# Checks of a DFT matrix by accumulating transfers, and gate weights kept in PSUM, in a Fourier-mixing and product-key expert kernel

## The chip, the cores and the metric

The kernel runs on one core of a Trainium2 chip. The metric is the device time of one execution in microseconds, and the median over executions is compared. The engines are TensorE (PE, with PEld for its weight loads), VectorE (DVE), ScalarE (ACT), GpSimd (POOL) and SyncE (SP). In this program SP issues nearly all transfers, in the order of its queue; POOL issues the transfers that add to what lies at their destination.

## What is computed

```python
xn = layernorm(x)                                  # 2048 x 512
a = einsum("bsd,ed->bse", xn, dft_hid_re)
b = einsum("bsd,ed->bse", xn, dft_hid_im)
y = einsum("ts,bse->bte", dft_seq_re, a) - einsum("ts,bse->bte", dft_seq_im, b)
q = einsum("nd,dhc->nhc", xn, w_q)                 # 32 heads, 2 x 128
s1, s2 = q1 . k1, q2 . k2                          # 64 keys each, top 2 of each
cand = t1[:, None] + t2[None, :]                   # top 2 of the 4 pairs, g = softmax
eidx = i1 * 64 + i2                                # one of 4096 experts
act = gelu(xn . u[eidx])
out = sum over heads and picks of g * act * v[eidx]
result = x + y + out
```

All matrices are inputs. The kernel uses the symmetries of the DFT matrices to load and multiply a quarter of them, and checks on the chip that the inputs have these symmetries. Where a check fails, it computes the general way at the end.

## The kernel before

A first part (to about 163 us) computes the Fourier mixing and stores its rows `y` in DRAM. A second part (to about 406 us) computes scores for eight chunks of heads and finds the two best keys of each half. The third part, which the change is in, goes through all 4096 experts for each of the 16 tiles of 128 tokens. Its phases alternate:

- **z**: `u` times the tokens gives one value for each expert and token, in PSUM, and gelu of it is written to `act`. From tile 2 on two tiles are done together, with seven products in place of eight. A list of 28 such products (`SEQ`, each 24 matmuls of 128 columns) sets their order. What comes out of each is copied by ACT (L1225, L1230, L1232), added by DVE (L1227, L1235, L1238) and passed through gelu by ACT (L1215). Three of the 28 are placed ahead of the phase, between the matmuls of the v phase before, and one behind it.
- **gates**: for 32 tokens at a time (`tg`, four per tile) DVE builds one-hot matrices `L` (L1279) and `R` (L1284, L1287), in three pairs of buffers, and PE multiplies them (L1289) into two banks `g`, of which there are two pairs. `w_part` then multiplies `act` by the gate (DVE, L1297) into an SBUF tile `w`, rounds it to f16 (ACT, L1304; in some places DVE, L1302) and keeps the rest as a second f16 number (DVE, L1305). Both halves overwrite `act`.
- **v**: for each tile, 16 groups of experts in eight slots, 12 matmuls of 512 columns each, add the output (L1349). Seven of the 16 groups of `v` come from DRAM in three buffers in turn.

The phases run z(0), z(1), v(0), then z(2,3), v(1), v(2), z(4,5), v(3), v(4) and so on. A z phase of a pair has 16 slots, a v phase 8. A table `plan` says what follows in program order behind the matmuls of each slot: `put(phase, slot, ...)`, with G for the gates' matmuls and W for `w_part`. A scheduling layer may move instructions against each other on an engine where nothing depends on it, except those that `pin` keeps in program order.

Between these phases lie the **checks**, which fill otherwise idle time and need nothing from the main work:

- 64 comparisons of C, the sequence DFT matrices. `compare` loads a base block of 128 x 128 and seven blocks of the same size that must equal it up to sign (448 KB, L1378). `compare_in` sums the base's magnitudes (DVE, L1385), subtracts or adds it (L1391, L1393, L1404), then mirrors (L1410). ACT sums the magnitudes of what is left over seven blocks (L1430). 16 of the 64 (those with `g == 0`) have special first rows.
- 4 comparisons of the hidden DFT matrices (`compare_w`, DVE L1457 to L1478, ACT L1480).
- 60 sums (`fit`) over weights, either loaded for it (L1488, L1496) or lying in SBUF (L1500), all on ACT.

Comparisons, loaded sums and the tiles `w` share one ring of four SBUF buffers (`WB = 4`). A comparison moves on by one stage with each slot that has a `U` or `F` in the plan:

```python
def step(it):
    for q in (later, loaded) if it is not None else (later, loaded, later):
        ready = q[:]
        del q[:]
        for f in ready:
            f()
    f = None if it is None else next(it, None)
```

The rows of `y` are loaded behind a v phase by SP (L1359), `x` is added by an accumulating transfer from POOL (L1360), DVE adds the scaled output (`finish`, L1364), and SP stores the result (L1365).

Of the kernel before, what the change touches and what calls it, by code (L numbers as in the profile page):

```python
# [36 lines left out]
def tile_fnet_peer(ctx, tc, x, ca, cb, c5, wt, wf, wr, wq, kt, ut, vn, out):  # L37
# [683 lines left out]
    def part_b(safe, stS, stP, stQ, stE, xt, u_sb, cmp_p, w4):  # L721
# [363 lines left out]
        WB = 4  # L1085
# [174 lines left out]
        GP = {}  # L1260

# [6 lines left out]
        def g_mm(b, tg):  # L1268
            cmp = CMP[b]
            p = pg(f"g{b}_{tg}")  # L1270
            for hf in range(2):
                ts = slice(tg * TG + hf * 16, tg * TG + hf * 16 + 16)

                def bc(w, n):
# [4 lines left out]
                nc.vector.tensor_tensor(  # L1279
                    L.rearrange("p t (l two) -> p t l two", two=2),  # L1280
                    io_lam.rearrange("p (l two) -> p l two", two=2).unsqueeze(1).to_broadcast([P, 16, P // 2, 2]),
                    bc(0, P), op=ALU.is_equal)
# [4 lines left out]
                nc.vector.tensor_tensor(Rv, Rv, bc(2, NC), op=ALU.mult)  # L1287
                for t in range(16):
                    nc.tensor.matmul(p[:, hf, t * NC:(t + 1) * NC], L[:, t, :], R[:, t, :], start=True, stop=True)  # L1289
            GP[b, tg] = p  # L1290

        def w_part(b, tg, here=False):
# [3 lines left out]
            w = bp.tile([P, NC, TG], F32, tag="w", name=f"w{b}_{tg}", bufs=WB)  # L1296
            nc.vector.scalar_tensor_tensor(w, act[:, :, ts], fw,  # L1297
                                           p.rearrange("p h (n c) -> p c (h n)", c=NC),
                                           op0=ALU.mult, op1=ALU.mult)
# [56 lines left out]

        def add_x(b):
            Y[b] = y = bp.tile([P, D], F32, tag="y", name=f"y{b}", bufs=1)
            nc.sync.dma_start(y, y_d[b])  # L1359
            nc.gpsimd.dma_start(y, x[b % 4, b // 4], accum_op=ALU.add)  # L1360

        def finish(b, pv):
            y = Y[b]
            nc.vector.scalar_tensor_tensor(y, pv, osc, y, op0=ALU.mult, op1=ALU.add)  # L1364
            nc.sync.dma_start(out[b * P:(b + 1) * P], y)  # L1365

        later, loaded = [], []
        pin = tc.keep_in_program_order

        def compare(n):  # L1370

            ri, g, kk = n // 32, n // 8 % 4, n % 8
            odd = kk // 4
            t = bp.tile([P, 4, 4, 64], F32, tag="w", name=f"cx{n}", bufs=WB)
            tf = t.rearrange("p s q c -> p (s q c)")
            tv = t.rearrange("p s q c -> p s (q c)")
            nc.sync.dma_start(tf[:, :P], ca[ri, g, :, kk * P:(kk + 1) * P])
            nc.sync.dma_start(tf[:, P:], cb[ri, g, kk].rearrange("p b c -> p (b c)"))  # L1378
            loaded.append(lambda: compare_in(n, t, tf, tv))

        def compare_in(n, t, tf, tv):

            ri, g, kk = n // 32, n // 8 % 4, n % 8
# [46 lines left out]
            later.append(lambda: pin(nc.scalar.activation(tf[:, P:], tf[:, P:], AF.Abs, accum_out=chk[:, n:n + 1])))  # L1430

        def compare_w(n):
# [3 lines left out]
            if n == 64:  # L1436
                r = bp.tile([P, 192], F32, tag="zb", name="wr")[0:1, 0:129]
                nc.sync.dma_start(r, wr)
                v = r[:, 2:128].rearrange("p (c a) -> p c a", a=2)
                pin(nc.vector.tensor_tensor(v, v, w2[0:1].unsqueeze(1).to_broadcast([1, 63, 2]), op=ALU.subtract))  # L1440
                nc.vector.tensor_tensor(r[:, 128:129], r[:, 128:129], w2[0:1, 1:2], op=ALU.subtract)
                later.append(lambda r=r: pin(nc.scalar.activation(r[:, 2:129], r[:, 2:129], AF.Abs, accum_out=chk[0:1, 70:71])))
            t = bp.tile([P, 4, 256], F32, tag="w", name=f"cx{n}", bufs=WB)
# [5 lines left out]
            loaded.append(lambda: compare_w_in(n, t))  # L1449

        def compare_w_in(n, t):

            ri, half = divmod(n - 64, 2)
            v = [t[:, k] for k in range(4)]
# [24 lines left out]
            f = t.rearrange("p k e -> p (k e)")[:, P - half * ri:]  # L1479
            later.append(lambda: pin(nc.scalar.activation(f, f, AF.Abs, accum_out=chk[:, n:n + 1])))  # L1480

        def fit(n):

            if n < NK:
                t = bp.tile([P, 2 * D], F32, tag="w", name=f"fit{n}", bufs=WB)
                nc.sync.dma_start(t.rearrange("p (h k) -> p h k", h=2), wq[1 + n // 4, n % 4 // 2, n % 2])
                loaded.append(lambda: later.append(
                    lambda: pin(nc.scalar.activation(t, t, AF.Abs, accum_out=fits[:, n:n + 1]))))  # L1488
                return
            g = n - NW  # L1490
            t = bp.tile([P, 2 * D], F32, tag="w", name=f"fit{n}", bufs=WB)
            if g >= 16 + V2:
                h = t.bitcast(F16)[:, 0:2 * D]
                nc.sync.dma_start(h, v_d[g - 16 - V2, :, 0:2 * D])
                loaded.append(lambda: later.append(
                    lambda: pin(nc.scalar.activation(h, h, AF.Abs, accum_out=fits[:, n:n + 1]))))  # L1496
                return
            src = (u_sb[g][:, 0].rearrange("p c k e -> p (c k e)") if g < 16 else
                   v_sb[g - 16][:, 0].rearrange("p c d -> p (c d)"))
            pin(nc.scalar.activation(t, src, AF.Abs, accum_out=fits[:, n:n + 1]))  # L1500

        def verdict():
# [37 lines left out]
        fit_units = [iter([lambda n=n: fit(n) for n in ns]) for ns in (  # L1540
            (*range(NK), *range(NW + 16 + V2, NW + 32)), range(NW, NW + 16 + V2))]
        units = iter([lambda n=n: (compare if n < 64 else compare_w)(n) for n in range(68)])

        def step(it):
            for q in (later, loaded) if it is not None else (later, loaded, later):
                ready = q[:]
                del q[:]
                for f in ready:
                    f()
            f = None if it is None else next(it, None)  # L1550
            if f is not None:
                f()
# [301 lines left out]
```

## Time and profile before

| | |
|---|---|
| time, median of 3 runs | 1132.39 us (1127.87 to 1136.62) |
| the profiled execution's own time | 1135.25 us |
| its span, first to last instruction | 1133.4 us |
| PE busy | 1107.3 us (98%) |
| DVE busy | 962.7 us (85%) |
| ACT busy | 663.9 us (59%) |
| POOL busy | 332.7 us (29%) |
| moved by DMA | 220.51 MB |
| mean granted clock of TensorE | 0.995 |

The span is 1.9 us shorter than the time of the same execution. Lines of the profile begin with `L` and the line of the kernel. A row of the view by lines ends with the busy time, the mean of one instruction in ns, and the idle time of the engine just ahead of these instructions with what ended it. In the view of waits each row gives the sum, the number and the longest.

### The profile page before, as it was taken

The numbers are of one execution on the slowest core, as the hardware profiler recorded it, in microseconds if no ns is written. First come the engines' busy times: TensorE is split into PE (matmuls) and PEld (weight loads), VectorE is DVE, ScalarE is ACT, GpSimd is POOL, SyncE is SP. The second block draws the span as 40 slices with busy tenths as digits, with TensorE's granted clock in tenths as the row PEclk, the third lists the DMA queues.
The fourth block names the chain that finished last, engine by engine and source line by source line (L and its number), as shares of the span: only waits on it lengthen the run. The fifth ranks groups of instructions, "written<-read, shape, count | busy, mean of one in ns | idle before, by whom it ended". The sixth has DMA issues, their size and how long they took to land.

```text
span 1133.4 us, 29112 instructions
## 1 busy us (share of the span) xinstructions
PE 1107.3 (98%) x11528; PEld 722.5 (64%) x11528; DVE 962.7 (85%) x2904; ACT 663.9 (59%) x1098; POOL 332.7 (29%) x385
## 2 busy tenths in 40 slices
PE   9999999999999999999999999999999999999997
PEld 6455554544545459687488478478569569569643
DVE  7899789999989799948997897898888888888793
ACT  6558598888877584346445545544535545544442
POOL 0429999899888850000000000000000000000000
PEclk9999999999999999999999999999999999999999
DMA  9883546465353335866666777666668668566354
GB/s 291 292 206 148 185 139 223 117 217 170 92 168 96 111 108 191 236 199 205 226 206 226 227 218 241 218 207 232 200 205 263 199 211 269 190 221 206 121 168 134
DMA packets 132273, 220.51 MB, mean 195 GB/s; under 512 B 35092, under 2 KB 71067, under 8 KB 132126
## 3 DMA queue, kind: packets, MB, share of 16 engines
q1 hardware_dynamic: 129520, 214.28, 58.7%
q0 software_dynamic: 2304, 4.20, 2.8%
q8 instruction: 92, 1.51, 0.5%
q14 instruction: 55, 0.45, 0.1%
q10 hardware_dynamic: 302, 0.08, 0.0%
HBM read 183.06 MB, written 29.69 MB: 188 GB/s over the span
## 4 chain that ended last, share of the span: by engine, by line
PE 59%; DVE 15%; DMA 5%; ACT 4%; issue 2%; POOL 1%; SPq 0%; ACTq 0%; DVEq 0%
PE s L252 18%; PE z L1186 17%; PE v L1349 16%; PE z L1108 4%; DMA cx<-in_cb_dram 3%; DVE w L1297 3%; DVE L L1279 3%; PE g L1289 3%; DVE act L1305 2%; PE m L148 1%; DVE R L1287 1%; DVE R L1284 1%; DVE w L1305 1%; DMA s<-s_d 1%; DVE cx L1393 1%
## 5 line engine op out<-in xcount | busy, mean ns | idle before, releaser
L252 PE MATMUL s<-m,xq 128*128 128x512 f16 x1344 | 297.4, 379 | 1.7 <-ACT ss L962 1.4
L1349 PE MATMUL v<-v,act 128*128 128x512 f16 x1044 | 233.3, 379 | 0.0
L252 PEld LDWEIGHTS <-xq 128*128 128x128 f16 x1344 | 129.6, 98 | 153.1 <-issue 3.2
L1360 POOL DMA_DIRECT2D y<-in_x_dram x16 | 14.4, 897 | 658.7 <-DMA v<-v_d 274.7
L1279 DVE TENSOR_TENSOR L<-io_lam,cmp 128x2048 f16<-128x2048 f16 x128 | 156.2, 1221 | 28.1 <-PE g L1289 28.1
L1349 PEld LDWEIGHTS <-act 128*128 128x128 f16 x1044 | 99.2, 98 | 112.4
L1186 PEld LDWEIGHTS <-u 128*128 128x128 f16 x2688 | 156.2, 98 | 14.8 <-issue 8.3
L966 DVE MAX8 vals<-ss 128x8 f32<-128x64 f32 x896 | 133.3, 216 | 5.5 <-ACT ss L962 5.2
L1186 PEld LDWEIGHTS <-s 128*128 128x128 f16 x1944 | 110.6, 98 | 1.2 <-DMA s<-s_d 1.2
L1349 PE MATMUL v<-v,w 128*128 128x512 f16 x480 | 109.0, 384 | 0.0
L1304 ACT ACTIVATE act<-w 128x1024 f16<-128x1024 f32 x36 | 48.9, 1358 | 92.2 <-DVE w L1297 92.2
L970 DVE FIND_INDEX8 idx<-vals,ss 128x8 uint16<-128x256 f32 x224 | 93.7, 418 | 0.0
L962 ACT ACTIVATE ss<-s,wsc 128x512 f32<-128x512 f32 x120 | 80.0, 680 | 22.5 <-PE s L252 12.6
L1186 PE MATMUL z<-xb,u 128*128 128x128 f16 x1344 | 84.9, 220 | 5.3 <-DVE w L1227 4.7
L1186 PE MATMUL z<-x,u 128*128 128x128 f16 x1344 | 84.7, 220 | 1.6 <-DVE act L1238 1.1
L1186 PE MATMUL z<-x,s 128*128 128x128 f16 x1296 | 81.2, 219 | 1.0 <-DMA s<-s_d 1.0
L1215 ACT ACTIVATE act<-act,scl 128x512 f32<-128x512 f32 x56 | 39.6, 720 | 70.9 <-DVE act L1235 40.9
L1349 PEld LDWEIGHTS <-w 128*128 128x128 f16 x480 | 46.1, 99 | 53.1 <-issue 2.3
L1430 ACT ACTIVATE cx<-cx 128x896 f32<-128x896 f32 x64 | 60.0, 938 | 29.6 <-DVE cx L1410 11.7
L1289 PEld LDWEIGHTS <-L 128*128 128x128 f16 x2048 | 60.7, 96 | 17.3 <-issue 7.2
L1289 PE MATMUL g<-R,L 128*128 128x32 f16 x2048 | 63.5, 177 | 6.6 <-DVE R L1287 6.2
L1305 DVE TENSOR_TENSOR act<-w,act 128x1024 f16<-128x1024 f32 x44 | 58.6, 1332 | 6.1 <-ACT act L1304 6.1
(363 smaller groups left out, 1878.9 us busy)
## 6 DMA issues: line engine op xcount, KB each, us to landing
v<-v_d SPq DMA_DIRECT2D x67, 512.0 KB, 4.6
s<-s_d SPq DMA_DIRECT2D x63, 512.0 KB, 4.2
cx<-in_cb_dram SPq DMA_DIRECT2D x64, 448.0 KB, 5.7
w<-in_wq_dram SPq DMA_DIRECT2D x28, 512.0 KB, 5.9
fit<-in_wq_dram SPq DMA_DIRECT2D x28, 512.0 KB, 4.3
uv<-in_vn_dram SPq DMA_DIRECT2D x16, 512.0 KB
uv<-in_ut_dram SPq DMA_DIRECT2D x16, 512.0 KB, 3.5
s_d<-v SPq DMA_DIRECT2D x32, 256.0 KB, 2.5
```

The source lines that it names most:

```text
L252: nc.tensor.matmul(ps, xt[i][:, l, kd, :], m[:, r, kd, :], start=(n == 0), stop=(n == 3 * KD - 1))
L962: nc.scalar.activation(s, ps, AF.Copy, scale=inv)
L966: nc.vector.max(vals[:, i, w, :, h], s[:, g, :])
L970: nc.vector.max_index(idx[:, i, w].rearrange("p k h -> p (k h)"), vals[:, i, w, 0:2].rearrange("p k h -> p (k h)"), s[:, w * HC:g + 1, :]. ...
L1108: nc.tensor.matmul(ps if n == 1 else ps.rearrange("p (b n) -> p b n", b=2), ug[:, l, c % 2, kd, :], xb2[:, k0, r, kd, :] if n == 1 else xb ...
L1186: nc.tensor.matmul(bank[:, t * P:(t + 1) * P], lt, rt, start=(t == k == 0 and op in "125"), stop=(t == 3 and k == 5), skip_group_check=op ...
L1279: nc.vector.tensor_tensor(L.rearrange("p t (l two) -> p t l two", two=2), io_lam.rearrange("p (l two) -> p l two", two=2).unsqueeze(1).to_ ...
L1289: nc.tensor.matmul(p[:, hf, t * NC:(t + 1) * NC], L[:, t, :], R[:, t, :], start=True, stop=True)
L1304: nc.scalar.activation(w16[..., 0], w, AF.Copy)
L1305: nc.vector.tensor_tensor(w16[..., 1], w, w16[..., 0], op=ALU.subtract)
L1349: nc.tensor.matmul(pv, w16[:, c, :, l], v_sb[g][:, r, cc, :], start=(n + cc == 0 and k == 0), stop=(n == end and cc == 1 and k == 2))
L1430: later.append(lambda: pin(nc.scalar.activation(tf[:, P:], tf[:, P:], AF.Abs, accum_out=chk[:, n:n + 1])))
```

## The change

**The comparisons.** For 48 of the 64 comparisons of C (those with `g` not 0) DVE no longer subtracts. `base_load` brings the base block alone into a small tile `cb` (three buffers). `expect` lets DVE sum its magnitudes (L1411) and lets ACT write the negated expectation of all seven blocks into the check's tile, in one to four instructions by a table of signs (`SETS`, L1418; a few more of one column each where `kk == 0`, L1422). Then POOL issues an accumulating transfer that adds the seven blocks of the input on top (L1423). `sum_up` sums the magnitudes of the result on ACT (L1428). The other 16 and the four of the hidden matrices work as before.

**The weights.** `w` is no longer an SBUF tile: L1307 writes the product back into the gates' own PSUM banks, and the rounding (L1312, L1310) and the rest (L1313) read it there. So a pair of banks is in use until the rest is taken. The ring of four buffers holds checks alone (`CB = 4`, tag `cx`).

**The building of L and R** is a function of its own (`g_prep`), put into the plan as `LRP` one to three slots ahead of its matmuls; G and W have new slots.

**A table of times.** The steps of a check are put at slots by a table: 2.1 us are counted for a slot of z and 3.0 us for a slot of v. The base is loaded 7 us ahead of `expect`, and the sum taken 9 us behind it. A comparison of the old kind is computed 8 us behind its load and summed 12 us behind. The 128 checks are spread evenly over the slots. `load_y`, `add_x` and `store` have slots of their own too.

```diff
-        def g_mm(b, tg):
+        def g_prep(b, tg):
...
-            p = pg(f"g{b}_{tg}")
...
+                PREP.setdefault((b, tg), []).append((L, R))
+                pin(nc.vector.tensor_tensor(
...
+        def g_mm(b, tg):
+            if (b, tg) not in PREP:
+                g_prep(b, tg)
+            p = pg(f"g{b}_{tg}")
+            for hf, (L, R) in enumerate(PREP.pop((b, tg))):
...
-            w = bp.tile([P, NC, TG], F32, tag="w", name=f"w{b}_{tg}", bufs=WB)
-            nc.vector.scalar_tensor_tensor(w, act[:, :, ts], fw,
-                                           p.rearrange("p h (n c) -> p c (h n)", c=NC),
-                                           op0=ALU.mult, op1=ALU.mult)
+            w = p.rearrange("p h (n c) -> p c (h n)", c=NC)
+            nc.vector.scalar_tensor_tensor(w, act[:, :, ts], fw, w, op0=ALU.mult, op1=ALU.mult)
...
+        def load_y(b):
+            Y[b] = bp.tile([P, D], F32, tag="y", name=f"y{b}", bufs=1)
+            pin(nc.sync.dma_start(Y[b], y_d[b]))
+
         def add_x(b):
-            Y[b] = y = bp.tile([P, D], F32, tag="y", name=f"y{b}", bufs=1)
-            nc.sync.dma_start(y, y_d[b])
-            nc.gpsimd.dma_start(y, x[b % 4, b // 4], accum_op=ALU.add)
+            pin(nc.gpsimd.dma_start(Y[b], x[b % 4, b // 4], accum_op=ALU.add))
...
+        SETS = {(0, 0): ((-1, 0, ((7, 1),)),),
...
+        def base_load(n):
+
+            ri, g, kk = n // 32, n // 8 % 4, n % 8
+            b = T[n, "b"] = bp.tile([P, 132], F32, tag="cb", name=f"cb{n}", bufs=3)
+            nc.sync.dma_start(b[:, :P], ca[ri, g, :, kk * P:(kk + 1) * P])
+            if kk == 0:
+                nc.sync.dma_start(b[:, P:P + 1], cb[ri, g, 0, :, 0, 0:1])
+
+        def expect(n):
...
+            t = T[n] = check_tile(f"cx{n}")[:, 0:7 * P].rearrange("p (h c) -> p h c", h=7)
+            pin(nc.vector.tensor_reduce(asum[:, n:n + 1], b[:, :P], axis=AX.X, op=ALU.add, apply_absolute_value=True))
+            for sign, at, dims in SETS[ri, kk // 4]:
...
+                pin(nc.scalar.activation(v, src.to_broadcast([P, *[k for k, step in dims], P]), AF.Copy, scale=float(sign)))
...
+            pin(nc.gpsimd.dma_start(t.rearrange("p h c -> p (h c)"), cb[ri, g, kk].rearrange("p b c -> p (b c)"),
+                                    accum_op=ALU.add))
+
+        def sum_up(n):
+            f = T.pop(n).rearrange("p h c -> p (h c)")
+            pin(nc.scalar.activation(f, f, AF.Abs, accum_out=chk[:, n:n + 1]))
...
-                put(ph, 1, G(b + 1, 0))
+                put(("v", b - 1), 7, LRP(b + 1, 0))
+                put(ph, 1, G(b + 1, 0), LRP(b + 1, 1))
...
-                for k in range(4):
-                    put(ph, 2 * k or b % 2, W(b + 1, k))
-                put(ph, b % 2, G(b + 1, 2))
-                put(ph, 3, G(b + 1, 3))
...
+                put(ph, 3, G(b + 1, 2), LRP(b + 1, 3))
+                put(ph, 4, W(b + 1, 2), G(b + 1, 3))
+                put(ph, 6, W(b + 1, 3))
...
+            kinds = [[((timed(base_load, n), -7.0), (timed(expect, n), 0.0), (timed(sum_up, n), 9.0))
+                      for n in range(64) if n // 8 % 4],
```

Two places in the built order. The first is DVE where v(7) ends and v(8) begins: `y` is the finish of v(7), L and R (with `cmp`) belong to the gates of tile 9, `cx` and `cb` to checks, `g_3` and `w_126` to the last weights of tile 8. Before:

```order
L1385 TENSOR_REDUCE sums<-cx_12484 128x1
L1418 COPY cx_12456<-cx_12456 1x128
L1391 TENSOR_TENSOR cx_12484<-cx_12484 128x256
L1393 SCALAR_TENSOR_TENSOR cx_12484<-cx_12484,not_79 128x256
L1287 TENSOR_TENSOR R_5773<-R_5773,cmp_12414 128x512
L1395 TENSOR_TENSOR cx_12484<-cx_12484 1x256
L1410 TENSOR_TENSOR cx_12484<-cx_12484 128x128
L1410 TENSOR_TENSOR cx_12484<-cx_12484 1x128
L1364 SCALAR_TENSOR_TENSOR y_12510<-v_12228,scl,y_12510 128x512
L1418 COPY cx_12484<-cx_12484 1x128
L1279 TENSOR_TENSOR L_5774<-io_lam,cmp_12414 128x2048
L1284 TENSOR_TENSOR R_5775<-io_c,cmp_12414 128x512
```

The same place on DVE in the changed kernel:

```order
L1307 SCALAR_TENSOR_TENSOR g_3_12403<-w_126,scl,g_3_12403 128x32x32
L1291 TENSOR_TENSOR R_5773<-R_5773,cmp_12378 128x512
L1283 TENSOR_TENSOR L_5774<-io_lam,cmp_12378 128x2048
L1313 TENSOR_TENSOR w_126<-g_3_12403,w_126 128x32x32
L1411 TENSOR_REDUCE sums<-cb_12440 128x1
L1283 TENSOR_TENSOR L_5772<-io_lam,cmp_12378 128x2048
L1291 TENSOR_TENSOR R_5775<-R_5775,cmp_12378 128x512
L1288 TENSOR_TENSOR R_5777<-io_c,cmp_12378 128x512
L1291 TENSOR_TENSOR R_5777<-R_5777,cmp_12378 128x512
L1373 SCALAR_TENSOR_TENSOR y_12297<-v_12232,scl,y_12297 128x512
L1283 TENSOR_TENSOR L_5776<-io_lam,cmp_12378 128x2048
L1283 TENSOR_TENSOR L_5772<-io_lam,cmp_12378 128x2048
```

Both halves of L and R for the first gates of tile 9 now stand ahead of the finish, and the operations of the comparison that stood there are gone but for one sum of the base.

The second place is ACT at the end of z(12,13): `z_12` are the banks of that phase, `act` the results of its two tiles, `w_0` or `g_0` the first weights, `cx` checks. Before:

```order
L1215 ACTIVATE act_14121<-act_14121,scl 128x4x128
L1232 ACTIVATE act_14299<-z_12_0_14726 128x4x128
L1215 ACTIVATE act_14121<-z_12_2_14532,scl 128x4x128
L1430 ACTIVATE cx_14792,sums<-cx_14792 128x896
L1215 ACTIVATE act_14299<-act_14299,scl 128x4x128 x2
L1215 ACTIVATE act_14121<-z_12_0_14726,scl 128x4x128
L1304 ACTIVATE act_14121<-w_0_15141 128x32x32
L1430 ACTIVATE cx_14971,sums<-cx_14971 128x896
```

The same place on ACT in the changed kernel, where `cb` is a base block:

```order
L1232 ACTIVATE act_14275<-z_12_0_14733 128x4x128
L1215 ACTIVATE act_14111<-z_12_2_14523,scl 128x4x128
L1428 ACTIVATE cx_14727,sums<-cx_14727 128x896
L1418 ACTIVATE cx_15094<-cb_14981 128x2x2x128
L1418 ACTIVATE cx_15094<-cb_14981 128x128
L1418 ACTIVATE cx_15094<-cb_14981 128x2x128
L1215 ACTIVATE act_14275<-act_14275,scl 128x4x128 x2
L1428 ACTIVATE cx_14881,sums<-cx_14881 128x896
L1428 ACTIVATE cx_15094,sums<-cx_15094 128x896
L1215 ACTIVATE act_14111<-z_12_0_14733,scl 128x4x128
L1312 ACTIVATE act_14111<-g_0_14759 128x32x32
```

One sum stood between two gelus of the phase's end; now three sums and three writes of an expectation stand there, and the last two sums wait for accumulating transfers.

More of the change, by code (lines that the diff above doesn't have):

```diff
@@ L1644, in part_b @@
[L1644 to L1649 removed]
+            slots = [(ph, cg) for ph in phases[2:] for cg in range(16 if len(ph) == 3 else 8)][:-5]
+            at = [0.0]
+            for ph, cg in slots:
+                at.append(at[-1] + (2.1 if ph[0] == "z" else 3.0))
@@ L1650, in part_b @@
+            put(("z", 1), 3, timed(load_y, 0))
+            put(("z", 1), 6, timed(add_x, 0))
         ZP = {}
```

204 lines of the change are left out of this document (120 added, 84 removed), and 3 rows, old and new, of the table SETS.

## The prediction

> **What bounds the kernel now.** I read the page first, then the waits of PE, then the timeline around its longest gaps, then the granted clock beside them.
>
> ```profile
> span 1133.4 us, 29112 instructions
> PE 1107.3 (98%) x11528; PEld 722.5 (64%) x11528; DVE 962.7 (85%) x2904; ACT 663.9 (59%) x1098; POOL 332.7 (29%) x385
> ...
> PE g L1289 <- DVE R L1287: 6.2, 10, 2.2
> PE z L1186 <- DVE w L1227: 4.7, 3, 2.4
> PE z L1186 <- DVE act L1238: 1.1, 1, 1.1
> PE z L1186 <- DMA s<-s_d: 1.0, 1, 1.0
> PE z L1186 <- DVE act L1235: 0.6, 2, 0.3
> PE z L1186 <- DVE act L1227: 0.3, 1, 0.3
> PE z L1186 <- DVE w L1235: 0.2, 1, 0.2
> ```
>
> PE is busy 98% of the span, and the change removes no matmul. So only PE's idle time can be won. In the third part PE waits 6.2 + 4.7 + 1.1 + 0.6 + 0.3 + 0.2 = 13.1 us for DVE, and 1.0 us for a load of `s`. It never waits there for ACT. Two of the longest waits, from the timeline:
>
> ```profile
> 773.11 0.88 DVE L1393 SCALAR_TENSOR_TENSOR cx<-cx,not 128x256 f32<-128x256 f32 x2 [2.08 <-DMA cx<-in_cb_dram]
> ...
> 774.37 0.67 DVE L1238 TENSOR_TENSOR act<-z,w 128x512 f32<-128x512 f32 x1
> ...
> 775.17 0.67 DVE L1227 TENSOR_TENSOR w<-z,w 128x512 f32<-128x512 f32 x1
> ...
> 775.89 1.50 PE L1186 MATMUL z<-xb,u 128*128 128x128 f16 x24 [1.97 <-DVE w L1227]
> ...
> 819.16 0.73 DVE L1364 SCALAR_TENSOR_TENSOR y<-v,scl,y 128x512 f32<-128x512 f32 x1
> ...
> 823.02 0.55 PE L1289 MATMUL g<-R,L 128*128 128x32 f16 x16 [2.24 <-DVE R L1287]
> ```
>
> In the first, DVE stands 2.08 us in front of a check whose transfer has not landed; two additions of z banks are queued behind it, and PE needs the bank. In the second the gates' R is late, since a run of comparisons and the finish stood ahead of it (the first order above). Both are DVE's queue, not DVE's total.
>
> ```profile
> 556.00:568.00 12.00, 10.19 (x93) 5.13 (x90) 11.35 (x21) 4.93 (x9) 0.86 (x1) 0.86 0.85 286
> 1040.00:1044.00 4.00, 3.85 (x66) 3.85 (x66) 1.68 (x4) 3.31 (x6) 0.00 (x0) 0.60 0.19 75
> 932.00:967.00 35.00, 35.00 (x690) 34.92 (x687) 29.82 (x49) 19.26 (x32) 0.86 (x1) 1.00 0.72 232
> ```
>
> Each row is a window with its length, the busy time of PE, PEld, DVE, ACT and POOL, and then the granted clock. Behind two of the waits the clock is granted in part: 12 x 0.14 = 1.7 us and 4 x 0.40 = 1.6 us are lost, 3.3 us in all. The Trainium skill, "TensorE: Matmul & The Clock Gate", Part 1, lets the clock drop only after an idle window of about 3.4 us. The trace differs: its longest wait is 2.4 us, and the clock fell. By the page the 3.3 us would not be on offer; I go by the rows.
>
> So what is on offer is 13.1 + 3.3 = 16.4 us, and 1.0 us of DMA.
>
> **DVE's share of the checks.** The subtractions and mirrors of 48 comparisons go:
>
> ```profile
> L1404 DVE TENSOR_TENSOR cx<-cx 128x512 f32<-128x512 f32 x36 | 24.6, 684 | 7.6 <-DMA cx<-in_cb_dram 7.6
> L1404 DVE TENSOR_TENSOR cx<-cx 128x256 f32<-128x256 f32 x36 | 15.0, 417 | 0.7 <-DMA cx<-in_cb_dram 0.7
> L1404 DVE TENSOR_TENSOR cx<-cx 128x768 f32<-128x768 f32 x12 | 11.4, 951 | 3.0 <-DMA cx<-in_cb_dram 3.0
> L1410 DVE TENSOR_TENSOR cx<-cx 128x128 f32<-128x128 f32 x56 | 15.7, 283 | 0.1
> ```
>
> All of L1404 is theirs, 24.6 + 15.0 + 11.4 = 51.0 us, and 42 of the 56 mirrors, 11.9 us: 63 us of DVE, with 11.3 us of waits for transfers. This is time beside PE, so it counts only through the 13.1 us. Twenty comparisons stay on DVE with their operations in one piece, now computed 8 us by the table behind their load. The waits of z phases behind checks sum to 4.7 + 1.1 + 0.6 + 0.3 + 0.2 = 6.9 us; I leave 20/68 of that, 2.0 us. Of the gates' 6.2 us I leave 0.6, since `LRP` puts all of L and R ahead of the finish, as the order shows. Gain: 13.1 - 2.6 = 10.5 us, and the 3.3 us of clock, as no wait near 2 us is left. The bounds are 0 and 16.4 us.
>
> **Weights in PSUM.** The three steps for one quarter tile, in the timeline:
>
> ```profile
> 546.81 1.27 DVE L1297 SCALAR_TENSOR_TENSOR w<-w,scl,g 128x1024 f32<-128x1024 f32 x1
> 548.12 1.35 ACT L1304 ACTIVATE w<-w 128x1024 f16<-128x1024 f32 x1 [4.81 <-DVE w L1297]
> 549.53 1.28 DVE L1305 TENSOR_TENSOR w<-w,w 128x1024 f16<-128x1024 f32 x1
> ...
> 483.80 2.59 PE v L1349 x12
> ...
> 581.49 6.71 PE z L1186 x120
> ```
>
> Before, the gates' banks came free at 548.08, now they come free at 550.81, 2.7 us later. In the plan W stands two slots of v or more ahead of the G that reuses its banks: 2 x 2.59 = 5.2 us against a chain of 4.0 us. So I cost it at nothing; the cover is 1.2 us, and if ACT's rounding is later than that, PE idles for the rest. The rounding on DVE has this row, and the multiplication that reads the strided banks already has the next:
>
> ```profile
> L1302 DVE CAST act<-w 128x1024 f16<-128x1024 f32 x8 | 6.0, 744 | 0.0
> L1297 DVE SCALAR_TENSOR_TENSOR w<-w,scl,g 128x1024 f32<-128x1024 f32 x20 | 25.5, 1274 | 5.8 <-ACT w L1215 5.8
> ```
>
> Read from PSUM, the 12 roundings on DVE cost between 744 ns each and 1274 ns, at most 12 x 0.53 = 6.4 us; I take the upper end, as it is the row with the same source. The Trainium skill, "VectorE: DVE Perf Modes", "Why PSUM operands drop a tier", speaks against the change here: an fp32 operand in PSUM takes a copy out of the double rate. No run so far shows it. It lies on DVE in z phases, which have 29.82 of 35 us busy, beside two gates built there; half a microsecond twice per phase is within the 2.6 us left above.
>
> **ACT's share.** Writing expectations has no row; these bound it:
>
> ```profile
> L1430 ACT ACTIVATE cx<-cx 128x896 f32<-128x896 f32 x64 | 60.0, 938 | 29.6 <-DVE cx L1410 11.7 <-DVE cx L1418 8.1 <-issue 5.8
> L1225 ACT ACTIVATE act<-z 128x512 f32<-128x512 f32 x16 | 9.5, 591 | 6.2 <-PE z L1186 6.2
> L1474 ACT ACTIVATE cx<-cx 1x128 f32<-1x128 f32 x2 | 0.6, 308 | 6.8 <-DVE cx L1472 5.9 <-ACT fit L1496 0.9
> ```
>
> A 256-wide one I put at 0.40, between 308 and 591 ns. The four kinds of expectation, 12 comparisons each, then take 0.94 (one of 896), 1.30 (512, 256, 128) twice, and 1.51 (three of 256 and one of 128): 12 x 5.05 = 61 us. ACT has the room on average, but the spread matters. In z(12,13), the window from 932 to 967, ACT was busy 19.26 of 35 us, with these among it:
>
> ```profile
> L1488 ACT ACTIVATE fit<-fit 128x1024 f32<-128x1024 f32 x2 | 2.1, 1052 | 0.0
> L1430 ACT ACTIVATE cx<-cx 128x896 f32<-128x896 f32 x2 | 1.9, 940 | 0.0
> ```
>
> That is 4.0 us of sums, at 0.94 us for a check's and 1.05 for a sum over weights. In the changed order there stand between the first copy of that phase and its last gelu four expectations (5.4 us), seven sums (6.6 us) and four sums of weights (4.2 us): 16.2 us. That stretch lasts 35 us and the first slot of v with the last product, 2.59 + 1.34, so (19.26 - 4.0 + 16.2) / 39 = 81% of ACT, from 55%. What ACT does for PE there has slack: a copy of product 1 must be done before product 6, two products (2 x 1.34 = 2.7 us) later, and takes 0.59. So ACT may be late by 2.1 us. An expectation and a weight sum together hold it for up to 1.51 + 1.05 = 2.6 us, 0.5 us too long; with each of some 25 expectations in z phases that would be 12.5 us, and with none 0. I take a third, 4 us of new PE idle time.
>
> **The transfers.**
>
> ```profile
> q1 hardware_dynamic: 129520, 214.28, 58.7%
> q0 software_dynamic: 2304, 4.20, 2.8%
> ...
> y<-in_x_dram POOLq DMA_DIRECT2D x16, 256.0 KB, 5.5
> ...
> DMA to landing us min/median/max: 4.2/5.5/8.3
> ```
>
> The last two rows are the accumulating transfers of `x`. Per MB, they hold the 16 engines for 0.028 x 1133 / 4.20 = 7.6 us, plain ones for 0.587 x 1133 / 214.28 = 3.1 us. The 48 x 448 KB = 22 MB that change over cost 22 x 4.5 = 99 us more of sixteen engines, over some 620 us: the share of DMA rises from about 0.70 to 0.86. One load of `s` was late by 1.0 us; I take 1.5 us more, bounds 0 and 6 (each of seven z phases late by 0.9). A landing of 448 KB has bounds of 5.5 + 0.75 x 2.0 = 7.0 us (only the 0.028 x 1133 / 16 = 2.0 us of packets grow) and 5.5 x 1.75 = 9.6 us (all grows). `sum_up` stands 9 us behind by the table, rounded up to a slot, so about 10.4 us; less 1.3 us of writing, that covers 9.1 us. I take the lower end, the same fixed path. On POOL, `add_x` and the expectations queue behind each other; with a transfer each 8 us or so they rarely meet. `load_y`, `add_x` and `store` moved cost nothing: `add_x` stands two slots of an even v ahead of its finish, with three products among them, and POOL can issue earlier. Without that cover, the finish waits up to 8.3 us at worst, with z additions behind it on DVE. SP loses 48 large issues to POOL and no longer stands in front of a store.
>
> **The sum**: -10.5 - 3.3 + 4 + 1.5 = -8.3 us. From the profiled execution's own 1135.25 us that gives 1127.0, from the median of 1132.39 us 1124.1. The profiled one lies 2.9 us over the median; I predict for the median: **1124 us**.
>
> **The rivals.**
> - *All of it goes*: ACT's slack takes everything, 13.1 + 3.3 us less 1 to 4 us, 1116 to 1120 us. For it: no wait of PE for ACT in the third part now. Against: ACT at 81% in z phases.
> - *Banks held*: the rounding comes behind an expectation and a sum (1.3 + 0.94 us), over the 1.2 us of cover by 1.0 us. 32 gates follow their W by two slots or three; a third of them late by 0.8 us gives 8 us: 1132, no change.
> - *Slower*: accumulating transfers land later than the cover of 9.1 us, and ACT, in order, stands at `sum_up` with the last gelu of the phase and the rounding behind it, as in the second order. At 11.6 us, 2.5 us late, 3.6 sums per z phase take 9 us of ACT, which has 7 free; PE loses some 4 us in each of seven phases: 1124 + 28 = 1152. It decides from about 10.5 us on. For it: the landing at 9.6 us if all grows, and 8.3 us already among the 16. Against: ten of the sums stand seven products or more behind.
>
> **How the numbers follow.** Forecast (1120 to 1129) 0.42, all of it 0.33, banks held 0.12, slower 0.13. A measurement here can tell about 1%, 11.3 us, so faster is below 1121 and slower above 1144. Faster: 0.33 and a little of the forecast, 0.35; slower 0.13; within 1% 0.52. Signs differ little in the likeliest case, whose own range is 1120 to 1129. For 8 in 10, the range goes from 1114, just under the first rival, to 1139, which takes in banks held and leaves out the slower one.
>
> **What would show it.** Right: waits of PE for DVE under 4 us in the third part, no half clock, DVE near 900 us busy, ACT near 725, the first waits of PE behind ACT (z behind L1225, L1232 or L1215). Banks held: PE's `g` waits for L1313. Slower: ACT's L1428 waits for `cx<-in_cb_dram`, with landings over 10 us. Wrong altogether if DVE's z additions are still late where no check is near.

## The result, and the profile after

The changed kernel takes 1165.3 us (median of 4 runs, 1162.96 to 1168.81) where the kernel before takes 1131.22: a ratio of 1.030, with a 95% interval of 1.025 to 1.035. It is 34 us slower, outside the predicted range.

The head of the page of the changed kernel, with its DMA queues:

```profile
span 1162.0 us, 29163 instructions
PE 1112.0 (96%) x11528; PEld 725.7 (62%) x11528; DVE 916.9 (79%) x2760; ACT 707.8 (61%) x1248; POOL 373.9 (32%) x433
...
q1 hardware_dynamic: 123472, 192.26, 51.3%
q0 software_dynamic: 9216, 26.22, 13.5%
```

DVE is busy 46 us less and ACT 44 us more; 63 less and 61 more had been forecast. The durations of the single instructions do add up to that (61 less on DVE, 63 more on ACT), but neighbouring instructions of one engine overlap a little in the records, so the busy time moves by less. PE, with the same 11528 matmuls, idles more. Its waits in the third part, longest in total first:

```profile
PE z L1186 <- ACT act L1232: 7.2, 2, 4.2
PE z L1186 <- DMA s<-s_d: 6.1, 5, 2.2
PE z L1186 <- DVE act L1235: 4.3, 3, 1.8
PE g L1299 <- DVE R L1291: 3.7, 5, 2.2
PE v L1357 <- DMA v<-v_d: 3.6, 1, 3.6
PE z L1186 <- ACT act L1215: 3.1, 1, 3.1
PE z L1186 <- DVE w L1238: 2.9, 1, 2.9
PE z L1186 <- DVE act L1238: 2.5, 2, 1.7
```

With the smaller rows these are 18.0 us for DVE (13.1 before), 10.3 for ACT (none before) and 9.7 for transfers (1.0 before). That is 24 us more, and PE's own busy time is 4.7 us longer for the same matmuls; together the 28.6 us by which the span grew. The longest sum of ACT's waits for a transfer, and then the landing of the loads of `v`, of `s` and of the accumulating transfers (KB each, median us to landing):

```profile
ACT cx L1428 <- DMA cx<-in_cb_dram: 61.8, 21, 6.1
...
v<-v_d SPq DMA_DIRECT2D x67, 512.0 KB, 3.8
s<-s_d SPq DMA_DIRECT2D x63, 512.0 KB, 5.4
cx<-in_cb_dram POOLq DMA_DIRECT2D x48, 448.0 KB, 7.2
```

The same loads in the kernel before:

```profile
v<-v_d SPq DMA_DIRECT2D x67, 512.0 KB, 4.6
s<-s_d SPq DMA_DIRECT2D x63, 512.0 KB, 4.2
```

By the median the loads of `s` land later than before and those of `v` earlier; single ones of both are waited for. ACT stands 61.8 us in front of sums whose transfer hasn't landed. One such place, from the timeline of the changed kernel around 1050 us:

```profile
1041.40 0.72 ACT L1215 ACTIVATE w<-w,scl 128x512 f32<-128x512 f32 x1 [7.29 <-DVE w L1227]
...
1047.59 1.22 ACT L1418 ACTIVATE cx<-cb 128x256 f32<-128x256 f32 x4
...
1049.22 0.86 POOL L1423 DMA_DIRECT2D cx<-in_cb_dram  x1 [12.57 <-ACT cx L1418]
...
1050.57 0.58 ACT L1230 ACTIVATE w<-z 128x512 f32<-128x512 f32 x1
...
1057.21 0.95 ACT L1428 ACTIVATE cx<-cx 128x896 f32<-128x896 f32 x1 [6.06 <-DMA cx<-in_cb_dram]
...
1058.16 0.58 ACT L1232 ACTIVATE act<-z 128x512 f32<-128x512 f32 x1
...
1058.78 1.73 PE L1186 MATMUL z<-x,s 128*128 128x128 f16 x24 [4.21 <-ACT act L1232]
```

The transfer takes 7.9 us from issue to landing. ACT is at its sum 2.3 us after the end of the expectation, waits 6.06 us, and the copy that PE needs is next in its queue. Going through all 48 in the trace, ACT reaches the sum between 0.7 and 25 us after the expectation (median 8.8), and the transfer lands 5.4 to 10.6 us after it (median 8.0). In 21 of the 48 ACT is there before the landing.

This looks like the whole story, and the first experiments were made on it. It turned out to be the smaller part.

### The profile page after: what moved, and what is told of

It reads as the page before. It is cut to its first block, busy times and chain, and to the rows that moved or that the text cites. A ratio compares the mean times of both kernels' runs of the same rounds, so it can differ in the third digit from the quotient of the medians.

```text
span 1162.0 us, 29163 instructions
## 1 busy us (share of the span) xinstructions
PE 1112.0 (96%) x11528; PEld 725.7 (62%) x11528; DVE 916.9 (79%) x2760; ACT 707.8 (61%) x1248; POOL 373.9 (32%) x433
## 3 DMA queue, kind: packets, MB, share of 16 engines
q1 hardware_dynamic: 123472, 192.26, 51.3%
q0 software_dynamic: 9216, 26.22, 13.5%
## 4 chain that ended last, share of the span: by engine, by line
PE 32%; DMA 11%; DVE 9%; issue 8%; ACT 2%; SPq 1%; POOL 0%; DVEq 0%; POOLq 0%; ACTq 0%
PE v L1357 18%; PE z L1186 12%; DMA cx<-in_cb_dram 5%; DMA s<-s_d 3%; PE g L1299 2%; DVE L L1283 2%; DVE g L1307 1%; DMA zt<-z_d 1%; DMA s_-1_6820<-s_d 1%; DVE R L1291 1%; DVE R L1288 1%; DMA z_d<-z 1%; DMA y<-y_d 0%; DVE act L1235 0%; DVE act L1313 0%
## 5 line engine op out<-in xcount | busy, mean ns | idle before, releaser
L1357 PE MATMUL v<-v,act 128*128 128x512 f16 x1044 | 236.1, 383 | 3.6 <-DMA v<-v_d 3.6
L1423 POOL DMA_DIRECT2D cx<-in_cb_dram x48 | 41.5, 865 | 500.3 <-ACT cx L1418 382.4
L1186 PEld LDWEIGHTS <-u 128*128 128x128 f16 x2688 | 159.0, 99 | 24.8 <-issue 18.4
L1428 ACT ACTIVATE cx<-cx 128x896 f32<-128x896 f32 (+1 forms) x68 | 64.2, 944 | 72.1 <-DMA cx<-in_cb_dram 61.8
L1312 ACT ACTIVATE act<-g 128x1024 f16<-128x1024 f32 x36 | 47.0, 1308 | 73.5 <-DVE g L1307 73.5
L1313 DVE TENSOR_TENSOR act<-g,act 128x1024 f16<-128x1024 f32 x44 | 57.1, 1301 | 20.5 <-ACT act L1312 20.2
L1307 DVE SCALAR_TENSOR_TENSOR g<-act,scl,g 128x1024 f32<-128x1024 f32 x44 | 55.9, 1284 | 14.5 <-ACT act L1215 14.5
```

The lines of the kernel that those rows point to most:

```text
L1186: nc.tensor.matmul(bank[:, t * P:(t + 1) * P], lt, rt, start=(t == k == 0 and op in "125"), stop=(t == 3 and k == 5), skip_group_check=op ...
L1307: nc.vector.scalar_tensor_tensor(w, act[:, :, ts], fw, w, op0=ALU.mult, op1=ALU.mult)
L1312: nc.scalar.activation(w16[..., 0], w, AF.Copy)
L1313: nc.vector.tensor_tensor(w16[..., 1], w, w16[..., 0], op=ALU.subtract)
L1357: nc.tensor.matmul(pv, w16[:, c, :, l], v_sb[g][:, r, cc, :], start=(n + cc == 0 and k == 0), stop=(n == end and cc == 1 and k == 2))
```

## The experiments

The theories, as the expectations name them: **A**, ACT in front of its sums; **B**, the traffic of the accumulating transfers delays other loads; **C**, the weights in PSUM; **D**, the table of times; **E**, SP's queue stands in front of loads of base blocks. Later **F**, the time for which accumulating packets hold the DMA engines; **G**, the bytes or POOL's issues; **H**, the adding transfer's own landing. Ratios are to the kernel before, measured beside each run.

### Later sums

```diff
-(timed(sum_up, n), 9.0))
+(timed(sum_up, n), 16.0))
```

> The changed kernel with the sum of an accumulated check put 16 us behind its expectation in the table, in place of 9. Theory A (ACT stands in its queue in front of sums whose accumulating transfer has not landed, 61.8 us in all, and copies and gelus of z are queued behind): ACT's waits for these transfers fall under 15 us, PE's waits for ACT from 10.3 us under 4, the time from 1165 to 1145 to 1155. Rival B (the accumulating packets take the DMA engines from the loads of s and v): the same number of transfers, so 1160 to 1168. Rival C (the weights held in PSUM): 1160 to 1168.

1160.98 us, 1.024 (1.019 to 1.029). The mechanism went as A expected and the time did not: ACT's waits for these transfers fell from 61.8 to 17.8 us, PE's waits for ACT from 10.3 to 3.1. But PE waits 18.4 us for DVE (18.0 in the changed kernel) and 12.0 for transfers (9.7). A alone isn't it.

### All comparisons in the old kind

```diff
-for n in range(64) if n // 8 % 4],
+for n in range(0)],
...
-for n in range(68) if not n // 8 % 4],
+for n in range(68)],
```

> The changed kernel with all 64 comparisons of C in the old kind: loaded whole by SP, subtracted by DVE 8 us behind the load by the table, summed by ACT 12 us behind it. No expectation and no accumulating transfer for checks; weights in PSUM, gates built ahead and the table stay. Theories A and B: ACT's 61.8 us and the late loads go, DVE is again over 950 us busy, 1130 to 1145. Rival C (weights in PSUM) or D (the table of times and the places of stores and loads): 1155 or more.

1149.72 us, 1.015 (1.011 to 1.018): between the two answers. One row explains it:

```profile
PE g L1299 <- DVE cx L1490: 14.2, 1, 14.2
```

At 456 us, where the third part has hardly begun, DVE stands in front of the first comparison with the R of a gate behind it. The same kernel with `first = 10` in place of 3 in the table, so that the first check stands seven slots later:

> All 64 comparisons of C in the old kind as in the earlier run, with the first check of all seven slots of the table later: in the earlier run one wait of 14.2 us stood behind the first comparison, at 456 us, before the third part has begun to go through its slots. That wait alone was in excess: 1132 to 1139. If the table of times costs more than that wait: 1143 or more.

1135.14 us, 1.002 (1.001 to 1.003). So with the first check later, weights in PSUM, gates built ahead and the table cost next to nothing together; C and D fall as causes of the 34 us.

### Only the weights in PSUM

The kernel before with this edit in `w_part`:

```diff
-w = bp.tile([P, NC, TG], F32, tag="w", name=f"w{b}_{tg}", bufs=WB)
-nc.vector.scalar_tensor_tensor(w, act[:, :, ts], fw,
-                               p.rearrange("p h (n c) -> p c (h n)", c=NC),
-                               op0=ALU.mult, op1=ALU.mult)
+w = p.rearrange("p h (n c) -> p c (h n)", c=NC)
+nc.vector.scalar_tensor_tensor(w, act[:, :, ts], fw, w, op0=ALU.mult, op1=ALU.mult)
```

> The kernel before with one edit: the product of weights and gates is written back into the gates' PSUM banks, and the rounding and the rest read it there. A, B and D: nothing over 1%, 1125 to 1143. C: the banks come free 2.7 us later and PE waits for them in the gates, 1145 to 1165.

1128.7 us, 0.996 (0.994 to 0.998): a gain of about 4 us, and the fastest kernel here that does all of the work. PE's waits for DVE fall from 13.1 to 6.7 us; those for the banks are short:

```profile
PE g L1289 <- DVE act L1303: 1.2, 4, 0.3
...
PE g L1289 <- DVE w L1303: 0.9, 3, 0.3
```

Is it that checks have the ring of four buffers to themselves (before, SP stands 39 us in front of loads of checks and of weights to sum, L1377 and L1486, for a release by L1305)? The ring cut to three:

> The kernel before with the weights in PSUM (1128.7 us) and with the ring of check buffers cut from four to three. Theory K (the gain of 4 us comes from the ring: SP no longer stands 39 us in front of check loads whose buffer a tile w still holds): about as the kernel before, 1130 to 1137, with DVE's waits for check transfers near 35 us again. Rival L (the gain comes from the weights' own steps in PSUM): 1126 to 1130.

1130.13 us, 0.997 (0.995 to 0.999). The time itself stands on the border of the two answers, but the kernel before, measured beside it, took 1133.76: 3.6 us of gain stay, though DVE waits 33 us for check transfers again (35 before, 22 with a ring of four). So most of it isn't the ring's length. Which of the weights' own steps it is stays open.

### Without the 48 accumulated checks

`range(64)` becomes `range(0)` in their list, and their columns of `chk` and `asum` are set once.

> The changed kernel without the 48 accumulated comparisons: their base loads, expectations, accumulating transfers and sums are left out, so these blocks of C are not compared. A and B: what they cost goes and with it also the relief of DVE is seen alone, PE waits under 12 us in the third part, 1115 to 1130. D (SP's queue with stores and loads by the table, and the 20 comparisons left on DVE) or C: 1140 or more.

1124.71 us, 0.992 (0.989 to 0.995). With DVE, ACT, POOL and SP all freed of these 48 checks, only 0.8% is gained, and part of that is the weights'. Under this plan it is the most that moving these 48 checks off DVE could have brought.

### Base loads kept in order

In the changed kernel SP stands 76.1 us (27 times) and 31.8 us (10 times) in front of base loads, since these are not kept in program order and moved forward to the release of a tile.

```diff
-nc.sync.dma_start(b[:, :P], ca[ri, g, :, kk * P:(kk + 1) * P])
+pin(nc.sync.dma_start(b[:, :P], ca[ri, g, :, kk * P:(kk + 1) * P]))
...
-nc.sync.dma_start(b[:, P:P + 1], cb[ri, g, 0, :, 0, 0:1])
+pin(nc.sync.dma_start(b[:, P:P + 1], cb[ri, g, 0, :, 0, 0:1]))
```

> The changed kernel with the loads of the base blocks kept in program order, which puts them behind the loads of s, v and checks that stand ahead of them in the table; in the changed kernel they had moved forward in SP's queue to just behind the release of a base tile. Theory E (SP stands 108 us in front of base loads whose tile is still held by the reduction on DVE or the expectation on ACT, with loads of s, v and checks queued behind): SP's waits of L1402 fall under 25 us, PE's waits for s and v from 9.7 us under 4, DVE's waits for checks from 28 us under 15, the time 1140 to 1155. Theory A (ACT in front of sums) or B (traffic) alone: 1160 to 1168.

1172.85 us, 1.040 (1.035 to 1.045). SP's waits of L1402 fall to 1.3 us, and the kernel is slower: expectations on ACT now wait 16.4 us for their base, and ACT waits 74.5 us at its sums. With the later sums too:

> Base loads in program order and the sums 16 us behind the expectation. If A and E both cost time and each hid the other in the single edits: 1125 to 1142. E alone: as with the base loads alone, within 3 us. B: 1155 or more.

1.042 (1.036 to 1.048). Neither gains, against E. But the edit trades one wait for another, since base loads now come later, so these two don't show by themselves that SP's 108 us are free. The run without transfers below does: SP stands 85 us there.

### Without the sums, and without the transfers

Two that separate A from B. In the first the 48 sums on ACT are left out (`timed(T.pop, n)` in their place).

> The changed kernel without the 48 sums of accumulated checks on ACT, so what these transfers leave isn't looked at; base loads, expectations and accumulating transfers stay where they are. A: ACT stands nowhere for a transfer and has 54 us less work, 1135 to 1150. E or B: 1155 or more, with SP's wait in front of base loads near 100 us.

1157.89 us, 1.023 (1.019 to 1.027). ACT waits for none of these transfers and is busy 43 us less (665.0 for 707.8; the durations alone add up to 54), and only some 8 us come back, with intervals that overlap a little. The largest waits of PE are now:

```profile
PE z L1186 <- DMA s<-s_d: 11.8, 8, 2.9
PE v L1357 <- DMA v<-v_d: 4.4, 2, 3.9
```

In the second the transfers themselves are left out.

> The changed kernel without the 48 accumulating transfers: base loads, expectations and sums stay, the sums are taken of the expectation alone and times zero, so these blocks are not compared. B and A: 1130 to 1148. E alone, or ACT's added work: 1155 or more.

1125.91 us, 0.996 (0.993 to 0.998). The same base loads (SP still stands 85 us in front of them, so E falls), the same expectations, the same sums, and all of the loss is gone. Next to the kernel without these checks (0.992), ACT's added work and SP's waits cost some 0.4%, with intervals that overlap. The loss comes with the 48 transfers: some 31 us of it (1.023 for 0.996) even where ACT looks at none of them.

### What of a transfer costs: plain, doubled, adding

The transfer stays at its place in POOL's queue, but writes instead of adding (no `accum_op`):

> The changed kernel with the 48 transfers from POOL's queue at the same places, but writing in place of adding; the sums are taken times zero, so these blocks are not compared. Theory F (an accumulating packet of 3584 bytes holds a DMA engine for 290 ns against 140 for a plain one, so loads of s, v and checks land late, and PE's waits of about 2 us bring the half clock): 1128 to 1145, landings of these transfers near 4 us. Rival G (the bytes, or the 48 issues from POOL's queue, whatever they do): 1150 or more.

1135.75 us, 1.0015 (1.000 to 1.003). The bytes and the issues cost some 6 us (0.6% more than without transfers); G falls. The adding costs 30 us. In the records of packets, one of 3584 bytes takes 291 ns (median) when it adds and 140 when it doesn't. To hold the engines as long without adding, a second plain transfer of the same bytes behind each, into a scratch area of DRAM:

```diff
+pin(nc.gpsimd.dma_start(sc_d[n], cb[ri, g, kk].rearrange("p b c -> p (b c)")))
```

> The kernel with 48 plain transfers from POOL's queue (1135.8 us), and behind each a second plain one of the same 448 KB from DRAM to DRAM, so that a check holds the DMA engines about as long as an accumulating transfer does (2 x 140 ns for 3584 bytes against 290 ns). The sums are taken times zero, so these blocks are not compared. Theory F (engine time, whatever holds it): 1150 to 1165, with waits of PE for s and v of 8 us or more. Rival H (the adding itself: its own later landing, in front of which ACT stands): 1134 to 1143.

1154.62 us, 1.021 (1.015 to 1.027). The four kernels side by side, each with its row of the window from 480 to 1110 us (busy us of PE, PEld, DVE, ACT and POOL, then clock, DMA share, GB/s). First without transfers, then plain, doubled and adding:

```profile
480.00:1110.00 630.00, 619.81 (x7934) 448.54 (x7933) 482.67 (x803) 363.00 (x664) 13.10 (x16) 1.00 0.57 181
```

```profile
480.00:1110.00 630.00, 616.48 (x7924) 449.02 (x7923) 484.53 (x801) 364.52 (x664) 39.14 (x63) 0.99 0.66 213
```

```profile
480.00:1110.00 630.00, 606.56 (x7832) 443.79 (x7829) 475.09 (x774) 359.93 (x658) 62.97 (x108) 0.99 0.73 244
```

```profile
480.00:1110.00 630.00, 597.43 (x7751) 439.44 (x7751) 462.98 (x754) 355.36 (x649) 51.05 (x59) 0.99 0.74 207
```

The second column of numbers, PE's busy time, falls as the share of the DMA engines rises. The doubled and the adding kernel hold them alike (0.73 and 0.74) though one moves 244 GB/s and the other 207. The loads of `s` land after 4.5, 4.9, 5.2 and 5.4 us (median) in the four. With plain transfers PE hardly waits for `s`; doubled, it does again:

```profile
PE z L1186 <- DMA s<-s_d: 0.6, 1, 0.6
```

```profile
PE z L1187 <- DMA s<-s_d: 7.1, 6, 2.3
...
PE v L1358 <- DMA v<-v_d: 1.2, 1, 1.2
```

From plain to doubled the ratio rises by 0.0195, some 22 us: F. The profiled execution of the doubled kernel is the fastest of its four, 8.6 us longer than the plain one, and 7.7 us of that are PE's waits for transfers; how the other 13 us of the medians come about, no profile shows. Doubling also adds bytes and issues, which the adding kernel does not. Against the bytes speaks that the packets of the loads, 4096 bytes each, take 159 ns (median) in all four kernels: the loads are not slower once they have an engine, they get it later.

From doubled to adding the ratio rises by 0.009, some 10 us, with intervals that overlap. That rest fits H: the plain transfer lands after 5.2 us there and the adding one after 7.2, ACT stands 27.6 us at these sums there and 61.8 with adding, and leaving out ACT's sums gave back 8 us.

### Fewer, in halves, and elsewhere

24 of the 48 accumulated, the others in the old kind:

```diff
-for n in range(64) if n // 8 % 4],
+for n in range(64) if n // 8 % 4 and n % 2],
...
-for n in range(68) if not n // 8 % 4],
+for n in range(68) if not n // 8 % 4 or n < 64 and n % 2 == 0],
```

> The changed kernel with 24 of the 48 checks accumulated and the other 24 subtracted on DVE as the 16 old ones are. If each transfer costs the same: half of the way between 1135 (all old, without the one wait at the start) and 1165, 1146 to 1153. If there is a threshold in the engines' time: 1140 or less.

1171.34 us, 1.034 (1.029 to 1.038), with the one wait at the start again (14.3 us). Without it, by `first = 10`:

> 24 of the 48 checks accumulated, with the first check seven slots later, which takes away the wait of 14.3 us at 456 us that stood in the earlier run too. Equal price of each transfer: between 1135 (none) and 1165 (48), so 1146 to 1155; a threshold: 1140 or less.

1155.23 us, 1.019 (1.014 to 1.025): 20 us for the first 24 transfers (from 1135), 10 for the next 24. So 24 are not free, and fewer were not run. Why the first 24 cost more than the next isn't shown; the checks also stand at other places.

Each transfer cut in two, 4.5 us apart, and the sum 13.5 us behind:

> The changed kernel with each accumulating transfer cut in two (four blocks, then three), the second 4.5 us behind the first, and the sum 13.5 us behind the expectation. F by the length of one burst (some 3 us of all engines, now half of it at a time): 1142 to 1156. F by the engines' total time: 1160 to 1170.

1219.53 us, 1.078 (1.074 to 1.083). This didn't test what it was made for. The second piece is issued late: in the trace, 43 of the 48 second pieces are issued 0.3 us after the first has landed, so the pieces go one behind the other and not 4.5 us apart. In the view of waits this stands as "issue", and ACT stands longer at its sums. The rows of POOL and of ACT:

```profile
POOL cx L1427 <- issue: 226.0, 47, 8.1
```

```profile
ACT cx L1432 <- DMA cx<-in_cb_dram: 126.2, 24, 13.0
```

With ACT standing that long, PE's waits rise to 51.5 us for DVE, 15.5 for ACT and 11.0 for transfers; what of it is ACT's part isn't shown, since the split changes more than that.

All 48 begun in slots of v, the other checks in slots of z:

> The changed kernel with all 48 accumulated checks begun in slots of v, and the other checks in slots of z, evenly in each. F with the loads of s in z as the place of the loss (z phases took 24 of the 36 us): 1140 to 1155. If the place doesn't matter, or ACT's roundings in v are held up as much as the gelus in z: 1160 to 1175.

1199.97 us, 1.059 (1.054 to 1.064). The same transfers, nearer to each other, come with twice the loss. ACT waits 139.5 us at its sums, and PE for the loads of v:

```profile
PE v L1357 <- DMA v<-v_d: 25.2, 10, 6.0
```

The other checks have moved too, so this isn't one cause alone; but what forecast a gain, that z phases are where it is lost, falls. PE's waits went from the loads of `s` (1.2 us here) to those of `v`, which run beside the transfers now.

## Why the prediction was wrong

**The bound.** PE's idle time was rightly named as all that could be won, and DVE's queue as its cause. But "13.1 - 2.6 = 10.5 us, and the 3.3 us of clock" was mis-sized. Without the 48 checks at all, the whole gain is 0.8% of 1132, 9 us, and 4 us are gained with the weights alone. The clock went as forecast in that kernel, with no half clock in the third part. But PE still waits 5.8 us for DVE where 2.6 were left: 2.6 us in z phases, near the 2.0 of the prediction, and 3.2 us in front of gates, where it left 0.6. Two of the z waits, at 870 and 957 us, come right behind stands of DVE for the transfer of an old comparison, which the 8 us of the table did not cover:

```profile
DVE cx L1457 <- DMA cx<-in_cb_dram: 21.0, 10, 4.3
```

**Weights in PSUM.** "I cost it at nothing": it gained 4 us. The cover holds: PE's waits for the banks are 0.3 us at most with the weights alone, and in the changed kernel PE waits for no bank at all. So the rival "banks held" falls. The upper end for the rounding was right:

```profile
L1310 DVE CAST act<-g 128x1024 f16<-128x1024 f32 x8 | 10.4, 1298 | 0.0
```

1298 ns against 744 from SBUF. That is as the Trainium skill says in "VectorE: DVE Perf Modes", "Why PSUM operands drop a tier". The read from the banks is strided as well, and no run here separates the two.

**ACT's share.** The durations were good, with 0.40 us put for this row:

```profile
L1418 ACT ACTIVATE cx<-cb 128x256 f32<-128x256 f32 x60 | 22.0, 406 | 0.0
```

ACT's busy time came to 707.8 us, not 725, since such neighbours overlap: the four instructions at 1047.59 above end after 1.22 us, though their durations add up to 1.5. PE's waits for ACT came to 10.3 us where 4 were taken. The reason given, 81% of ACT busy, was not the cause: without the transfers the same work leaves 2.4 us of such waits. The wrong step here is "that covers 9.1 us". As a median it was right (8.8), but the spread from 0.7 to 25 us was not in the sum, and ACT stood 61.8 us. The table spaces a sum from its expectation in slots of PE, while ACT has waits in its own queue. At 1041.40 us ACT had waited 7.3 us for an addition of DVE; the expectation of 1047.59 came behind that, and its sum soon after.

**The transfers.** This is the step that failed: "I take 1.5 us more, bounds 0 and 6" for late loads, where holding the engines that long cost some 22 us by the doubled kernel, and ACT's stands at the sums some 8 to 10 us more. The terms that led up to it were about right or too high. The landing was bounded by 7.0 and 9.6 us from issue; measured were 5.0 to 10.3, with a median of 7.2, next to the lower end that was taken. The time on the engines was put at 4.5 us per MB more, where the page gives 0.135 x 1162 / 26.22 - 0.513 x 1162 / 192.26 = 2.9. So the share of DMA, which the sum had rise from 0.70 to 0.86, rose from 0.66 to 0.74, and even that was too much. The row of the kernel before, for the window of the four rows above:

```profile
480.00:1110.00 630.00, 615.77 (x7895) 446.87 (x7894) 523.59 (x916) 316.50 (x507) 12.11 (x14) 0.99 0.66 211
```

An average share under 1 says nothing of a load of `s` that is issued when a buffer comes free and must land within a few us: its median went from 4.2 to 5.4 us, and the kernel had little slack for it, as the one wait of 1.0 us before already suggested.

**Stores and loads moved "cost nothing".** Nearly so, but for the end: the last loads of `v` now stand behind SP's reading of the flags (in the kernel before they stood ahead of it), and SP stands 18.0 us there. The flags come when the last check is summed. In front of stores (L1376) SP still stands 27 us, where the prediction had none; it was 75 us before.

```profile
1137.46 0.14 DVE L1604 TENSOR_SCALAR flag<-ok 1x1 int32<-1x1 f32 x1
...
1138.76 1.09 SPq L1333 DMA_DIRECT2D v<-v_d  x2
...
1142.27 1.01 PE L1357 MATMUL v<-v,act 128*128 128x512 f16 x2 [3.58 <-DMA v<-v_d]
```

With plain transfers SP's queue has the same order, and PE doesn't wait. The flags come 24 us before the end of the span in both kernels, but with the adding transfers 3.58 us of these are the wait.

**The clock.** The 3.3 us that were to be won here were not: PE's busy time grew by 4.7 us. Windows of 4 us of the changed kernel, each just behind a wait of PE: of 3.04 us at 506, 1.85 at 792, 3.08 at 870, 2.21 at 1000 and 4.21 at 1054:

```profile
508.70:512.70 4.00, 3.93 (x71) 3.93 (x71) 3.09 (x5) 4.00 (x9) 0.87 (x1) 1.00 0.21 64
...
794.00:798.00 4.00, 3.94 (x89) 3.94 (x89) 3.75 (x10) 3.23 (x6) 0.00 (x0) 1.00 0.81 304
873.10:877.10 4.00, 3.94 (x38) 3.94 (x38) 1.11 (x2) 3.59 (x8) 0.71 (x1) 0.50 0.65 110
...
1002.70:1006.70 4.00, 3.96 (x33) 2.06 (x33) 3.97 (x6) 2.71 (x5) 0.86 (x1) 1.00 0.43 94
...
1058.70:1062.70 4.00, 3.92 (x47) 3.92 (x47) 1.38 (x2) 4.00 (x11) 0.00 (x0) 0.65 0.30 79
```

The third-last number is the clock: full in three rows, a half and 0.65 in the others. Here waits of about 2 us left the clock alone, and of the waits near 3 us and above the first did too and the others shown didn't. The prediction went by the kernel before, where waits of 1.81 and 2.40 us had been followed by the half clock, against the figure of about 3.4 us of the Trainium skill, "TensorE: Matmul & The Clock Gate", Part 1. With plain transfers it was 0.57 over the 4 us behind one of 2.17 us. So no one length of wait decides it in these runs.

**The rivals.** Of the signs named for the forecast, PE's waits behind ACT came (L1232 and L1215), but its waits for DVE were 18.0 us instead of under 4, and the half clock stayed. "Slower" had the right sign, with a chance of 13%, and part of the right place: ACT at `sum_up`, decided by a landing from 10.5 us on, 1152. That point was wrong: the landing stayed under it (10.3 us at most), and ACT stood nonetheless, since the cover was often shorter than the table's. The larger part, late loads of `s` and `v`, stood in no rival.

## What to carry to other kernels

A DMA share of 0.66 was not a third of room here: what counted was whether the loads that PE waits for had slack in their landing, and added engine time on transfers went against that slack at once. Work moved from a vector engine to an accumulating transfer is paid in DMA engine time, here twice that of a plain one, so the first question is whether the loads beside it are early enough to bear that. And a delay that a planner counts in slots of one engine holds for that engine; a wait in another engine's queue must be read from where that engine really comes to it.

## What the runs showed of the hardware

An adding packet of 3584 bytes held a DMA engine for 291 ns (median of 6144) where a plain one took 140, and one of 2048 bytes 178 against 84: twice the time at both sizes. 448 KB landed after 7.2 us adding and 4.9 plain from the same queue, and its issue held POOL for 865 ns adding and 542 plain (medians). A rise of the DMA share from 0.66 to 0.73, by 48 more plain transfers, came with 2% more time, while in the kernel without the adding transfers waits of 85 us in SP's queue left the time under that of the kernel before (0.996).
